# A pinned instruction order carried on into batch 2 and arranged anew, with tile addresses from a list: slot attention and a GELU feed-forward layer on one core

## The chip, the core and the metric

The kernel runs on one NeuronCore of a Trainium2 chip. The core has a matrix engine (TensorE, PE in the rows, PEld for its weight loads), a vector engine (VectorE, DVE), a scalar engine (ScalarE, ACT), GpSimd (POOL) and SyncE (SP). Here SP issues nearly all DMA transfers. The metric is the device time of one execution in microseconds (us); less is better. The time of a kernel is the median of its runs.

## The reference

```python
# batch 8, heads 8, seq 576, head_dim 64, n_mem 32; float32, the weights float64
a = phi - np.max(phi, axis=2, keepdims=True)          # over seq
a = np.exp(a)
a = a / (np.sum(a, axis=2, keepdims=True) + 1e-09)
k_m = np.einsum('bhsm,bhsd->bhmd', a, k)
v_m = np.einsum('bhsm,bhsd->bhmd', a, v)
scores = (1.0 / np.sqrt(64)) * np.matmul(q, k_m.transpose(0, 1, 3, 2))
scores = scores - np.max(scores, axis=-1, keepdims=True)
attn = np.exp(scores)
attn = attn / (np.sum(attn, axis=-1, keepdims=True) + 1e-09)
x = np.matmul(attn, v_m)           # -> (4608, 512), heads side by side
h = x @ w_in                       # w_in (512, 2048)
g = 0.5 * h * (1.0 + erf(h / np.sqrt(2.0)))
out = g @ w_out                    # w_out (2048, 512)
```

The weights reach the core as 64-bit numbers, in two 32-bit halves, and are turned into float32 there.

## The kernel before

Each batch is 576 tokens. The attention part makes, per batch, a softmax over the sequence, 32 slots for each head (k_m and v_m) and the attention weights of the tokens over the slots. The feed-forward part never builds x: the slots v_m are first multiplied with w_in (tile U), and the hidden layer is attention weights times U. Every large product is made of three passes with operands split into a high and a low part (hi, lo).

The program is written as a list of small pieces. A piece is a name with numbers; `a`, `d` or `p` behind a colon puts it on ACT, DVE or POOL. The order of the pieces in the list is the order of the instructions on every engine, since a dependency is added from each instruction to the one before it on its engine. The pieces that the text speaks of:

- Loads, all on SP: `Lphi` (phi), `Lkv0`, `Lkv` (k and v), `Lq` (q), `Lwi.f` and `Lwo.f` (128 columns of w_in, 128 rows of w_out; f from 0 to 15). `os` stores a result.
- Softmax over the sequence, batch b, half of the heads g: `amax.b.g` (DVE), `aexp.b.g` (ACT), `anorm` (DVE), `at.b.g.c` (transposes on PE), `atc.b.g.c` (their copy out of PSUM).
- Slots: `slots.b.g` (PE), `km.b.g` (scaled copy), `slotsT` (PE), `kT` (copy). In batch 0 a third number says k (0) or v (1).
- Attention weights of batch 0, in three parts x: `n_score` (PE), `n_max`, `n_sub` (DVE), `n_exp` (ACT), `n_sum`, `n_inv`, `n_mul` (DVE), `n_T` (PE), `n_hi` (ACT), `n_lo` (DVE). In later batches `score`, `sT`, `max`, `sub`, `exp`, `sum`, `inv`, `mul`, `pT`, `ph`, `pl`.
- U: `Up.b.f.n` (PE), `Uh` (copy of the high part), `Ul` (DVE, the rest).
- Weights: `dB.f.k` (ACT, two instructions; k is 0 for w_in, 1 for w_out), `dC`, `dG`, `dS` (DVE), `dDi`, `dDo` (POOL), `dE` and `dF` (high and low part of w_out).
- Hidden layer: `h.b.f.hf` (PE, 6 matmuls, half the tokens), `gelu` (ACT), `gh` (high part, ACT or DVE), `gl` (low part, DVE), `p.b.f` (PE, 12 matmuls into acc), `o` (evict). From batch 2 on `P` and `O` with half batches. `tg`, `tp`, `to` do the same for the 64 tokens of a batch that are left over. `W` is a matmul whose result nobody reads.

`START` is the part of the list that is written out by hand; before, it ends with `p.1.15`, the last product of batch 1. What follows is put in order by a small planner (`put` with a due time, `run` after each `h`), which leaves out what `START` has done (`done`). `HOME` says which buffer (U0 to U4, kv0 to kv7, wy0, wy1) each big tile uses; a tile waits until the last reader of the tile that had the buffer before is through. Eight semaphores serve SP's transfers in turn, so that the ninth after a transfer isn't issued before that one has landed.

PE's names in the rows: pt = `at`, pk = `slots`, tn = `slotsT`, psc = `n_score` and `score`, pu = `Up`, pT = `n_T`, acc = `p`.

Of the kernel before, what the change touches and what calls it, by code (L numbers as in the profile page):

```python
# [50 lines left out]
n_max.1 n_sub.1 n_exp.1 n_mul.0 Lkv0.1.1 slots.0.1.1 Lphi.1.0 amax.1.0 n_sum.1 Lwi.2
km.0.1.1 Lphi.1.1 n_inv.1 n_mul.1 dDi.0 Lwo.2 slotsT.0.1 kT.0.1 aexp.1.0 Up.0.0.1
Lkv.1.0.0 dDi.1 dB.2.0 Uh.0.0:d Ul.0.0 dC.2.0 amax.1.1 aexp.1.1 dG.2.0 dS.2.0 Lkv.1.0.1
n_score.2 Up.0.1.1 Uh.0.1:d Lkv.1.0.2 Lwo.3 n_T.0 n_T.1 Ul.0.1 dDi.2 Lkv.1.0.3 n_max.2
n_sub.2 dB.2.1 dG.2.1 dC.2.1 at.1.1.0 dS.2.1 n_hi.0 at.1.0.0 Lkv.1.0.4 n_lo.0 h.0.0.0
atc.1.1.0 Lkv.1.1.0 atc.1.0.0:d at.1.0.4 n_exp.2 n_sum.2 n_inv.2 n_mul.2 atc.1.0.4:d
dB.3.1 n_hi.1 dC.3.1 dDo.2 dG.3.1 dS.3.1 dDo.3 anorm.1 at.1.1.4 n_T.2 atc.1.1.4
gelu.0.0.0 n_hi.2 Lwi.3 slots.1.0 km.1.0 Lkv.1.1.1 n_lo.2 n_lo.1 h.0.0.1 dB.3.0 dC.3.0
dS.3.0 dE.2 Up.0.2.1 Lkv.1.1.2 gelu.0.0.1 Lwo.4 Uh.0.2 Lkv.1.1.3 h.0.1.0 gelu.0.1.0
h.0.1.1 dG.3.0 dF.2 Ul.0.2 gh.0.0:a gl.0.0 dB.4.1 dC.4.1 dG.4.1 Lkv.1.1.4 slots.1.1  # L60
h.0.2.0 dS.4.1 km.1.1 slotsT.1 kT.1:d Lwi.4 dDi.3 Lwi.5 Lq.1.0 gelu.0.1.1 gh.0.1:a
dB.4.0 h.0.2.1 Up.0.3.1 p.0.0 gl.0.1 dE.3 dG.4.0 dDo.4 dE.4 dF.4 gelu.0.2.1 Uh.0.3
# [6 lines left out]
dG.6.1 dDi.6 Up.0.6.1 Uh.0.6 ph.1.0:d dC.7.1 h.0.5.0 h.0.5.1 dB.7.0 Ul.0.6 dC.6.1
max.1.1 dG.7.0 gelu.0.5.1 gelu.0.5.0 Up.1.0.4 Uh.1.0 dC.7.0 dS.7.0 sub.1.1 h.0.6.0  # L70
gelu.0.6.0 Lphi.2.1 dDi.7 amax.2.1 gh.0.5:a Ul.1.0 gl.0.5 pl.1.0 exp.1.1 dS.6.1 dDo.6
dE.6 h.0.6.1 gelu.0.6.1 p.0.4 Up.0.7.1 Uh.0.7:d sum.1.1 dS.7.1 inv.1.1 p.0.5 gh.0.6:a
Ul.0.7 Up.1.4.4 h.0.7.0 gelu.0.7.0 h.0.7.1 gelu.0.7.1 dG.7.1 Uh.1.4 mul.1.1 pT.1.1
ph.1.1:d dDo.7 dF.6 dB.8.1 h.1.0.0 gl.0.6 dE.7:d dF.7 p.0.6 dB.8.0 Lwo.9 dB.9.1 pl.1.1
# [1150 lines left out]
```

## Time and profile before

| | |
|---|---|
| median of 3 runs | 703.3 us (702.92 to 704.18) |
| the profiled execution | 704.61 us |
| its span, first to last instruction | 702.8 us |
| mean granted TensorE clock in it | 0.981 of full speed |
| busy in the span | PE 98%, PEld 82%, DVE 55%, ACT 42%, POOL 7% |

The span lies 1.81 us below the time of the same execution. A busy share is an average over the whole span; the first 40 us are quite different from the rest. Matmuls are pipelined and their ends are modelled, so how fast PE works is read from the distance of their starts.

### The profile page before, as it was taken

The numbers are of one execution on the slowest core, as the hardware profiler recorded it, in microseconds if no ns is written. First come the engines' busy times: TensorE is split into PE (matmuls) and PEld (weight loads), VectorE is DVE, ScalarE is ACT, GpSimd is POOL, SyncE is SP. The second block draws the span as 40 slices with busy tenths as digits, with TensorE's granted clock in tenths as the row PEclk, the third lists the DMA queues.
The fourth block names the chain that finished last, engine by engine and source line by source line (L and its number), as shares of the span: only waits on it lengthen the run. The fifth ranks groups of instructions, "written<-read, shape, count | busy, mean of one in ns | idle before, by whom it ended". The sixth has DMA issues, their size and how long they took to land.

```text
span 702.8 us, 12357 instructions
## 1 busy us (share of the span) xinstructions
PE 691.1 (98%) x4940; PEld 576.6 (82%) x4940; DVE 388.6 (55%) x705; ACT 298.4 (42%) x768; POOL 46.6 (7%) x39
## 2 busy tenths in 40 slices
PE   7999999999999999999999999999999999999997
PEld 5767787887878888888887888888877888888886
DVE  4989998954755366534943346433834346432222
ACT  4588766862615264524553224222531225322220
POOL 1232243310000000000000000000000000000000
PEclk7599999999999999999999999999999999999999
DMA  8954451416253571145600200020000200000001
GB/s 318 329 211 172 154 197 62 133 29 212 86 142 117 177 217 23 65 137 159 190 1 32 82 2 31 1 98 1 30 1 31 83 1 31 1 31 0 31 1 45
DMA packets 30716, 64.37 MB, mean 92 GB/s; under 512 B 3780, under 2 KB 8644, under 8 KB 30660
## 3 DMA queue, kind: packets, MB, share of 16 engines
q1 hardware_dynamic: 30564, 63.46, 27.6%
...
q10 hardware_dynamic: 96, 0.13, 0.1%
...
## 4 chain that ended last, share of the span: by engine, by line
PE 94%; DMA 1%; DVE 1%; SPq 0%; ACT 0%; issue 0%
PE acc L895 50%; PE h L855 29%; PE tacc L895 6%; PE pu L598 4%; PE psc L598 1%; PE psc L506 1%; DMA raw<-w_in 1%; PE pk L531 1%; PE x L506 1%; SPq L345 0%; PE pk L506 0%; PE psc L519 0%; PE psc L560 0%; DVE aT L210 0%; PE x L519 0%
## 5 line engine op out<-in xcount | busy, mean ns | idle before, releaser
L855 PE MATMUL h<-p_hi,U 128*128 128x288 f32 x1024 | 203.8, 298 | 0.0
L895 PE MATMUL acc<-wo_hi,gh 128*128 128x512 f32 x512 | 200.6, 392 | 0.0
L895 PE MATMUL acc<-wo_hi,gl 128*128 128x512 f32 x512 | 199.7, 390 | 0.0
L895 PE MATMUL acc<-wo_lo,gh 128*128 128x512 f32 x512 | 199.6, 390 | 0.0
L867 ACT ACTIVATE gf<-h 128x256 f32<-128x256 f32 x192 | 74.0, 387 | 265.0 <-issue 206.4
L855 PEld LDWEIGHTS h<-p_hi,U 128*128 128x128 f32 x1024 | 164.0, 188 | 23.0 <-issue 8.3
L210 DVE CAST gh<-gf 128x512 fp32r<-128x512 f32 x109 | 46.9, 430 | 167.4 <-ACT gf L867 165.3
L895 PEld LDWEIGHTS acc<-wo_hi,gh 128*128 128x128 f32 x512 | 96.5, 188 | 21.1 <-DVE gl L882 3.4
L895 PEld LDWEIGHTS acc<-wo_hi,gl 128*128 128x128 f32 x512 | 96.1, 188 | 21.5 <-DVE gl L882 0.9
L895 PEld LDWEIGHTS acc<-wo_lo,gh 128*128 128x128 f32 x512 | 96.1, 188 | 15.8
L855 PE MATMUL h<-p_lo,U 128*128 128x288 f32 x512 | 108.8, 294 | 0.1
L882 DVE TENSOR_TENSOR gl<-gf,gh 128x512 fp32r<-128x512 f32 x128 | 94.3, 736 | 15.2 <-ACT gh L210 5.7
L855 PEld LDWEIGHTS h<-p_lo,U 128*128 128x128 f32 x512 | 81.4, 188 | 0.6 <-DVE p_lo L693 0.6
L814 DVE TENSOR_TENSOR U<-pu,U 128x512 fp32r<-128x512 f32 (+2 forms) x50 | 40.8, 834 | 42.0 <-ACT U L210 41.8
L869 ACT ACTIVATE tails<-h 128x32 f32<-128x32 f32 x192 | 37.4, 195 | 0.0
L598 PE MATMUL pu<-w_in_sb,kT 64*32 64x512 f32 (+2 forms) x624 | 34.4, 528 | 0.4 <-ACT kT L210 0.4
L210 ACT CAST U<-pu 128x512 fp32r<-128x512 f32 (+2 forms) x42 | 30.4, 759 | 7.4 <-PE pu L598 7.3
L305 POOL TENSOR_TENSOR w_in_sb<-y,raw 128x512 int32<-128x512 int32 x16 | 23.8, 1493 | 43.8 <-DVE y L285 11.8
L305 POOL TENSOR_TENSOR y<-y,raw 128x512 int32<-128x512 int32 x16 | 21.9, 1374 | 56.5 <-DVE y L285 23.9
L272 ACT ACTIVATE y<-raw 128x512 f32<-128x512 f32 x32 | 21.6, 675 | 8.9 <-issue 4.3
L895 PE MATMUL tacc<-wo_hi,gh_t 128*128 128x512 f32 x64 | 25.0, 391 | 0.0
L895 PE MATMUL tacc<-wo_hi,gl_t 128*128 128x512 f32 x64 | 24.9, 389 | 0.0
...
## 6 DMA issues: line engine op xcount, KB each, us to landing
...
```

The source lines that it names most:

```text
L210: return e.copy(dst, src) if e is nc.scalar else e.tensor_copy(dst, src)
L272: nc.scalar.activation(y, high.bitcast(F32), AF.Abs, scale=2.0**16)
L305: nc.gpsimd.tensor_tensor(w, y, low, op=ALU.add)
L506: nc.tensor.matmul(pk[32 * j : 32 * j + 32, : 2 * D], st["aT", b][:, c, g, 32 * j : 32 * j + 32], st["kv", b, g, c][:, :, j, :], start=(c ...
L531: nc.tensor.matmul(pk[32 * j : 32 * j + 32, w0 * D : (w0 + n) * D], st["aT", b][:rows, c, g, 32 * j : 32 * j + 32], t[:rows, w0 : w0 + n, ...
L598: nc.tensor.matmul(ps[g][M * j : M * j + M], st["kT", b][rows, t, M * j : M * j + M], moving[j][rows], start=True, stop=True,)
L814: nc.vector.tensor_sub(u[:, ..., 1, :], pu, u[:, ..., 0, :].bitcast(F32))
L855: i = nc.tensor.matmul(h[:, :HS], u[g][w], x[:, g, :], start=(n == 0), stop=(n == 3 * G - 1))
L867: nc.scalar.activation(gf[:, f % 2 * n : f % 2 * n + n], h[:, :n], AF.Gelu)
L869: nc.scalar.activation(t, h[:, n:HS], AF.Gelu)
L882: nc.vector.tensor_tensor(g_of("gl", *k), g_of("gf", *k), g_of("gh", *k).bitcast(F32), op=ALU.subtract)
L895: nc.tensor.matmul(acc, x, w[:, f, :], start=(first and n == 0), stop=(last and n == 2))
```

## The change

`START` gets a new order from its first piece to `p.1.15` and goes on through the first half of batch 2 (850 pieces against 694). `PLACES` is new: a list of all tile tags with size and number of buffers, allocated in this order at the start, so that every tile has an address that doesn't depend on which piece comes first. `HOME` is the same. The pair `a_add`, `a_x` is now named apart, and the store `os` is a piece of its own and no longer the end of `o`. The entries of `st` that send some products to the accumulators' PSUM banks stand ahead of `START`, since it now reaches the pieces that use them. Over the whole program DVE has 675 rows for 685 and ACT 755 for 745: ten rows more move from DVE to ACT than back; PE's are the same ones in another order.

```diff
+PLACES = """
+kT:1024*3 phi:4608*1 nm:8*2 sm:8*2 aT:5120*1 rz:8*2 mx:72*2 smx:72*2 U0:8192*1 U4:8192*1
...
 START = """
-W.4.3 Lphi.0.0 amax.0.0 aexp.0.0 at.0.0.0 Lphi.0.1 amax.0.1 aexp.0.1 anorm.0 atc.0.0.0:d
...
+Lphi.0.1 Lphi.0.0 Lwo.0 Lkv0.0.0 Lkv0.1.0 Lq.0.0 Lwi.0 amax.0.0 Lwo.1 amax.0.1 aexp.0.1 Lq.0.1
...
+gl.0.0 km.1.1 dC.4.0 p.0.0 dB.4.1 dS.4.0 dC.4.1 gelu.0.1.0 dS.4.1 dG.3.0 amax.2.0 dDi.3
...
-    def first_tiles():
-
-        for tag in ("mx", "smx"):
-            sb.tile([P, G * SB], F32, tag=tag, name=f"{tag}_first")
+    for x in PLACES.split():
+        tag, size, n = x.replace("*", ":").split(":")
+        sb.tile([P, int(size) // 4], F32, tag=tag, name=f"place_{tag}", bufs=int(n))
...
-        if f == NF - 1 and j % 2:
-            r = b * S + (j - 1) * P
-            nc.sync.dma_start(
-                out[r : r + 2 * P, :].rearrange("(c p) n -> p c n", p=P), st["o", b, j // 2]
-            )
+
+    def store(b, j):
+        r = b * S + (j - 1) * P
+        nc.sync.dma_start(
+            out[r : r + 2 * P, :].rearrange("(c p) n -> p c n", p=P), st["o", b, j // 2]
+        )
```

First place: ACT at the start, behind its first table load and the load's exponential. phi is the softmax's input (`aexp`), aT the copy of a transpose (`atc`), y and raw the weights (`dB`), km the slots' copy. Before:

```order
L398 ACTIVATE phi_101,sm_105<-phi_101,nm_103 128x576 x2
L210 COPY aT_107<-pt_1_0_120 128x4x128
L272 ACTIVATE y_171<-raw_130 128x512
L273 ACTIVATE raw_130<-raw_130 128x512
L549 ACTIVATE km_201<-pk_0_144,rz_117 128x64
L549 ACTIVATE km_201<-pk_1_180,rz_117 128x64
```

and now:

```order
L414 ACTIVATE phi_136,sm_157<-phi_136,nm_152 128x576 x2
L288 ACTIVATE y_168<-raw_139 128x512
L289 ACTIVATE raw_139<-raw_139 128x512
L228 COPY aT_162<-pt_1_4_181 64x128
L228 COPY aT_162<-pt_1_0_163 128x4x128
L228 COPY aT_162<-pt_0_0_171 128x4x128
L561 ACTIVATE km_241<-pk_0_193,rz_217 128x64
L561 ACTIVATE km_241<-pk_1_219,rz_217 128x64
```

Two of the copies were DVE's, and all three now stand behind `dB.0.1`. The `x2` of the first row are `aexp.0.0`, `aexp.0.1` before and `aexp.0.1`, `aexp.0.0` now, while DVE has `amax.0.0`, `amax.0.1` in both and SP now loads group 1 first.

Second place: PE between the scores of batch 0 and the first products of U (`slots.0.g.1`, `slotsT.0.1`, `n_score.2`, `Up`). Before:

```order
L295 MATMUL warm_251<-one 128x128
L531 MATMUL pk_0_144<-kv_0_135,aT_107 32x64 x16
L531 MATMUL pk_0_144<-kvt_0_136,aT_107 32x64 x4
L531 MATMUL pk_1_180<-kv_1_139,aT_107 32x64 x16
L531 MATMUL pk_1_180<-kvt_1_140,aT_107 32x64 x4
L560 MATMUL tn_215<-ident,km_201 128x128
L598 MATMUL pu_0_330<-w_in_sb,kT_217 32x128 x8
L615 MATMUL psc_2_355<-k_blocks,q_1_169 128x2x32 x4
L598 MATMUL pu_1_360<-w_in_sb,kT_217 32x128 x8
```

and now:

```order
L543 MATMUL pk_1_219<-kv_1_145,aT_162 32x64 x16
L543 MATMUL pk_1_219<-kvt_1_146,aT_162 32x64 x4
L543 MATMUL pk_0_193<-kv_0_141,aT_162 32x64 x16
L543 MATMUL pk_0_193<-kvt_0_142,aT_162 32x64 x4
L627 MATMUL psc_2_357<-k_blocks,q_1_159 128x2x32 x4
L572 MATMUL tn_246<-ident,km_241 128x128
L610 MATMUL pu_0_386<-w_in_sb,kT_250 32x128 x8
```

`n_score.2` (psc_2) has moved ahead of `slotsT.0.1` (tn), and the unread matmul (warm) has moved to an earlier place. Behind this PE now has `n_T.0`, `Up.0.1.1`, all of `at.1`, `n_T.1`, the two short transposes, `h.0.0.0`, `slots.1.0`, `n_T.2`, `Up.0.2.1`, `h.0.0.1`, `slots.1.1`, `h.0.1.0` and then `p.0.0`; before, `h.0.1.1`, `h.0.2.0`, `slotsT.1`, `h.0.2.1` and `Up.0.3.1` still stood ahead of `p.0.0`, and `n_T.2` and the short transposes ahead of `slots.1.0`.

Third place: ACT and DVE up to the first low part, gl_0 (`gl.0.0`); gf and tails are `gelu`, gh is `gh`, p_hi_1 from pT_2 is `n_hi.2`, p_lo_1 from pT_2 is `n_lo.2`. ACT before:

```order
L873 ACT_TABLE_LOAD
L873 ACTIVATE gf_0_455<-h_0_0_415 128x288
L689 CAST p_hi_1_438<-pT_2_451 128x64 x2
L549 ACTIVATE km_481<-pk_0_460,rz_448 128x2x64
L272 ACTIVATE y_435<-raw_372 128x512
L273 ACTIVATE raw_372<-raw_372 128x512
L210 CAST wo_hi<-y_343 128x512
L875 ACTIVATE gf_0_455<-h_1_0_489 128x224
```

and now:

```order
L561 ACTIVATE km_526<-pk_0_495,rz_461 128x2x64
L701 CAST p_hi_1_486<-pT_2_528 128x64 x2
L885 ACT_TABLE_LOAD
L885 ACTIVATE gf_0_559<-h_0_0_473 128x288
L887 ACTIVATE gf_0_559<-h_1_0_548 128x224
L888 ACTIVATE tails<-h_1_0_548 128x64
L228 CAST gh_0_589<-gf_0_559 128x512
```

DVE now, from `n_lo.2` to `gl.0.0`:

```order
L705 TENSOR_TENSOR p_lo_1_487<-pT_2_528,p_hi_1_486 128x64 x2
L228 CAST U_0_395<-pu_2_535 128x2x128
L826 TENSOR_TENSOR U_0_395<-pu_2_535,U_0_395 128x2x128
L408 TENSOR_REDUCE nm_557<-phi_480 128x1
L228 CAST wo_hi<-y_364 128x512
L327 TENSOR_TENSOR wo_lo<-y_364,wo_hi 128x512
L293 TENSOR_SCALAR y_381<-y_381 128x512
L301 TENSOR_SCALAR y_381<-y_381 128x512
L894 TENSOR_TENSOR gl_0_606<-gf_0_559,gh_0_589 128x512
```

The table load and the first `gelu` stand behind `km.1.0` and `n_hi.2`, where they stood ahead of both. On DVE `Uh.0.2`, `amax.2.1` and `dE.2` are new between `n_lo.2` and `gl.0.0`.

## Rows read from the trace of the kernel before

**Rows 1.** The page: busy times, and the granted clock in 40 slices (tenths).

```profile
PE 691.1 (98%) x4940; PEld 576.6 (82%) x4940; DVE 388.6 (55%) x705; ACT 298.4 (42%) x768; POOL 46.6 (7%) x39
PEclk7599999999999999999999999999999999999999
```

**Rows 2.** Windows: stretch, length, busy time (instructions) by engine, granted clock, DMA share, GB/s.

```profile
0.00:10.20 10.20, 6.59 (x54) 5.86 (x57) 4.33 (x12) 5.04 (x9) 0.95 (x7) 1.00 0.80 255
10.20:34.10 23.90, 21.36 (x246) 17.65 (x234) 18.67 (x41) 11.14 (x26) 6.85 (x5) 0.50 0.96 350
34.10:37.50 3.40, 2.02 (x10) 1.01 (x8) 3.30 (x10) 2.70 (x8) 1.31 (x1) 1.00 0.35 142
37.50:41.00 3.50, 3.49 (x44) 2.63 (x45) 1.73 (x8) 2.74 (x7) 1.29 (x1) 0.51 0.34 118
41.00:60.00 19.00, 19.00 (x206) 14.82 (x205) 18.32 (x35) 16.95 (x37) 6.38 (x5) 1.00 0.81 297
60.00:80.00 20.00, 20.00 (x167) 14.34 (x166) 19.62 (x40) 14.98 (x30) 6.73 (x5) 1.00 0.13 41
```

**Rows 3.** The chain that ended last: start, length, what (two of its `p` groups).

```profile
47.40 2.99 PE acc L895 x12
...
244.77 2.72 PE acc L895 x12
```

**Rows 4.** Timeline, the start: start, length, instruction, idle time before and its releaser.

```profile
4.37 0.78 ACT L398 ACTIVATE phi<-phi,nm 128x576 f32<-128x576 f32 x1 [2.14 <-DVE nm L392]
4.59 0.75 DVE L392 TENSOR_REDUCE nm<-phi 128x1 f32<-128x576 f32 x1 [0.25 <-DMA phi<-phiT]
...
7.22 0.58 ACT L210 COPY aT<-pt 128x512 f32<-128x512 f32 x1 [0.97 <-PE pt L423]
...
9.83 0.78 PE L531 MATMUL pk<-kv,aT 128*32 128x64 f32 x32 [2.43 <-DMA kv<-kv]
...
15.07 7.06 PE L615 MATMUL psc<-k_blocks,q 128*128 128x64 f32 x32 [0.72 <-ACT k_blocks L210]
```

**Rows 5.** Timeline from the scores of batch 0 to the first hidden product.

```profile
22.59 1.08 PE L531 MATMUL pk<-kv,aT 128*32 128x64 f32 x32
...
26.57 0.27 ACT L210 COPY kT<-tn 128x128 f32<-128x128 f32 x1 [0.57 <-PE tn L560]
...
27.59 1.97 PE L615 MATMUL psc<-k_blocks,q 128*128 128x64 f32 x8
...
30.95 0.66 ACT L272 ACTIVATE y<-raw 128x512 f32<-128x512 f32 x1
...
32.08 0.68 ACT L689 CAST p_hi<-pT 128x288 fp32r<-128x288 f32 x2
...
33.57 0.76 PE L855 MATMUL h<-p_hi,U 128*128 128x288 f32 x2
...
34.50 0.42 ACT L646 ACTIVATE s<-s 128x256 f32<-128x256 f32 x1
```

**Rows 6.** Timeline from the slots of batch 1 on.

```profile
37.48 1.28 ACT L873 ACT_TABLE_LOAD   x1
37.51 2.52 PE L531 MATMUL pk<-kv,aT 128*32 128x128 f32 x40
38.77 0.41 ACT L873 ACTIVATE gf<-h 128x288 f32<-128x288 f32 x1
39.08 0.32 ACT L689 CAST p_hi<-pT 128x64 fp32r<-128x64 f32 x2
39.96 0.85 PE L855 MATMUL h<-p_hi,U 128*128 128x288 f32 x2
...
41.38 0.45 PE L598 MATMUL pu<-w_in_sb,kT 64*32 64x128 f32 x16
41.76 0.53 PE L855 MATMUL h<-p_hi,U 128*128 128x288 f32 x2
...
43.59 1.43 PE L531 MATMUL pk<-kv,aT 128*32 128x128 f32 x40
44.95 0.53 PE L855 MATMUL h<-p_hi,U 128*128 128x288 f32 x2
```

More of the change, by code (lines that the diff above doesn't have):

```diff
@@ L51 @@
[L51 to L62, printed above, removed]
@@ L69 @@
[L69 to L74, printed above, removed]
@@ new lines @@
+aexp.0.0 at.0.1.0 dB.0.1 at.0.0.0 dC.0.1 W.4.3 at.0.0.4 at.0.1.4 dS.0.1 Lwi.1 atc.0.1.4:a
+dG.0.1 atc.0.1.0 atc.0.0.0:a Lkv0.1.1 atc.0.0.4:d dDo.0 slots.0.0.0 dE.0:d W.4.13 anorm.0
+slots.0.1.0 dF.0 km.0.0.0 Lkv0.0.1 km.0.1.0 slotsT.0.0 W.3.29 kT.0.0 n_score.0 dB.0.0 Lwi.2
+dC.0.0 dG.0.0 dB.1.1 Lphi.1.0 dC.1.1 dS.1.1 dG.1.1 n_score.1 dS.0.0 dDo.1 n_max.0 n_sub.0
+dDi.0 n_exp.0 dE.1:a n_sum.0 dB.1.0 Lwo.3 dF.1 slots.0.1.1 Lwi.3 dC.1.0 Lphi.1.1 n_max.1 Lwo.2
+slots.0.0.1 dS.1.0 km.0.1.1 Lkv.1.1.2 dG.1.0 Lkv.1.0.0 n_inv.0 dDi.1 n_score.2 Lkv.1.0.3
@@ new lines @@
+dB.2.0 n_sub.1 amax.1.0 Lkv.1.0.4 km.0.0.1 dC.2.0 n_exp.1 slotsT.0.1 n_mul.0 Lkv.1.1.0 kT.0.1
+dB.3.1 n_sum.1 Up.0.0.1 n_T.0 dC.3.1 Lkv.1.0.2 n_inv.1 Uh.0.0:a aexp.1.0 Ul.0.0 Lwi.4 n_max.2
+Up.0.1.1 amax.1.1 n_sub.2 Uh.0.1:a Lkv.1.0.1 dS.3.1 aexp.1.1 Ul.0.1 Lkv.1.1.1 n_exp.2 n_mul.1
+at.1.0.0 dB.2.1 Lwo.4 dS.2.0 dC.2.1 at.1.1.0 dG.3.1 atc.1.0.0:a n_T.1 dG.2.0 atc.1.1.0 anorm.1
+n_hi.0 dDi.2 at.1.1.4 at.1.0.4 n_lo.0 h.0.0.0 Lphi.2.1 atc.1.0.4:a atc.1.1.4 n_sum.2 n_hi.1
+dDo.3 n_lo.1 dB.3.0 slots.1.0 n_inv.2 dS.2.1 Lkv.1.1.3 dE.3 n_mul.2 Lkv.1.1.4 dG.2.1 km.1.0
@@ new lines @@
+n_T.2 Lwo.5 n_hi.2 Up.0.2.1 Lphi.2.0 n_lo.2 dDo.2 h.0.0.1 Uh.0.2:d Ul.0.2 amax.2.1 gelu.0.0.0
+slots.1.1 Lwo.6 gelu.0.0.1 dE.2:d Lwi.5 gh.0.0:a dF.2 Lq.1.0 h.0.1.0 dC.3.0 dB.4.0 dS.3.0
+gl.0.0 km.1.1 dC.4.0 p.0.0 dB.4.1 dS.4.0 dC.4.1 gelu.0.1.0 dS.4.1 dG.3.0 amax.2.0 dDi.3
+slotsT.1 kT.1:d h.0.1.1 dF.3 Lwo.7 Up.0.3.1 dG.4.0 gelu.0.1.1 gh.0.1:a h.0.2.0 dG.4.1 dDi.4
+Uh.0.3 h.0.2.1 Ul.0.3 gelu.0.2.0 gl.0.1 dB.5.1 score.1.0 dDo.4 dB.5.0 p.0.1 sT.1.0.1 sT.1.0.0
+max.1.0 gelu.0.2.1 Lwo.8 dE.4 dC.5.0 Lwi.6 dC.5.1 gh.0.2:a Lq.1.1 sub.1.0 Lwi.8 Up.0.4.1
@@ L1000, in slot_attention_gelu_ffn @@
     }
+    st.update({("far", "pu", b, f): 1 for b in range(3, B) for f in (4, 12)})
+    st.update({("far", "psc", b, 1): 1 for b in range(3, B)})
+    st.update({k: 1 for k in (("far", "xt", 3), ("far", "pu", 2, 12))})
     done = set()
@@ L1167, in slot_attention_gelu_ffn @@
             if end:
-                behind += [f"o.{b}.{j}.{f}" for j in range(NT)]
+                for j in range(NT):
+                    behind += [f"o.{b}.{j}.{f}"]
+                    if f == NF - 1 and j % 2:
+                        behind += [f"os.{b}.{j}"]
         else:
```

124 lines of the change are left out of this document (66 added, 58 removed).

## The prediction

> **What bounds the kernel now.** I read the page first: PE is busy for 98% of the span, and its clock is below full speed in the first slices only [rows 1]. Since ends of matmuls are modelled, a busy PE need not be a fast one, so I looked next at the windows and at the distance of starts. From 41 us on PE has no idle time in any window and the granted clock is full [rows 2]. One `p` group of 12 matmuls takes 2.99 us at 47 us and 2.72 us at 245 us [rows 3]: there is some friction while the weights are decoded, and none later. So behind 41 us there is nothing to wait for that a better order could take away. It can only add waits there.
>
> The gain has to come from the first 41 us, and the windows show what they look like. From 10.2 to 34.1 us the clock is granted at half (1.2 GHz), 3.4 us are at full speed, and from 37.5 to 41 us it is half again [rows 2]; PE had paused for `h.0.0.0` and the transposes ahead of the second fall. In this part DVE is the engine with the least air: busy 18.67 of 23.9 us from 10.2 on, 3.30 of 3.40 us from 34.1 on, and 19.62 of 20 us between 60 and 80 us [rows 2]. So PE and DVE are close to each other for the first 90 us, and the time is set by when PE's steady stream begins and whether DVE then keeps ahead of it. The pieces behind p.1.15 and all of batch 2 lie in the part without waits: that `START` reaches further, that stores are pieces of their own and that addresses come from a list I cost at nothing, hidden behind a PE that is never idle; if that cover were gone, a store or a load costs its place on SP only.
>
> **The start, up to the scores.** Before, the first `aexp` begins at 4.37 us and the second `amax` at 4.59 us, when the second load has landed [rows 4]. Now group 1 is loaded first, but DVE still takes `amax.0.0` first, which has to wait for the second load; ACT takes `aexp.0.1` first. So ACT starts at 4.59 + 2 x 0.75 = 6.1 us, and two exponentials of 0.78 us end at 7.7 us, where before the second ended at about 4.59 + 0.75 + 0.78 = 6.1 us: 1.6 us later. Before, the last long copy ended at 7.22 + 0.58 = 7.8 us, and `slots.0.0.0` still waited until 9.83 us for its load [rows 4]. Now there are 1.6 us more, and two copies that DVE did beside ACT stand in ACT's row (0.58 us and a short one of about 0.3), all behind `dB.0.1`: 7.8 + 1.6 + 0.9 = 10.3 us at least. I take 11.1, because the copy that is needed is the last of the three and the first of them waits for the last short transpose. The cover by the load is used up, and PE is 1.3 us late. I give back 0.2 us, an estimate, for the unread matmul that no longer stands ahead of `slotsT.0.0`. So the scores start at 16.2 us for 15.07 us [rows 4].
>
> **From the scores to the first hidden product.** The two scores take 7.06 us [rows 4], to 23.2 us. Before, it took 3.98 us from the first of the two `slots` to `kT.0.1` (22.59 to 26.57 us); now `n_score.2` stands between (1.97 us) and covers the pause for `km` (I take 0.8 us of it): `kT.0.1` comes at 28.3 us for 26.57 us [rows 5]. Behind it ACT has `dB.3.1`, whose first half (0.66 us) releases DVE's `dC.3.1`, `n_inv.1`, `Ul.0.0`, `n_max.2` and `amax.1.1`: six instructions at DVE's mean in this stretch, 18.67 / 41 = 0.46 us [rows 2], together 2.7 us. Then ACT has `aexp.1.1` (0.78 [rows 4]), `n_exp.2` (0.42), `dB.2.1` (two halves, 1.2), two copies (1.1) and `n_hi.0` (0.68) [rows 4, 5]: 4.2 us. With kT's own 0.27 us that is 7.8 us, so `h.0.0.0` starts at 36.1 us, 2.5 us later than the 33.57 us of before [rows 5].
>
> Most of this comes back at once. Before, the short transposes and `n_T.2` stood between `h.0.0.0` and `slots.1.0`, which began at 37.51 us [rows 6]. Now only the low part stands there: two DVE instructions (0.9 us) and the last two matmuls, so `slots.1.0` begins at about 37.3 us. At half clock it takes 39.96 - 37.51 = 2.45 us [rows 6], and `n_T.2` behind it about 0.5 us, an estimate: at 40.2 us PE has done what it had done at 39.96 us before. **First term: +0.2 us.** Its bounds are -1.3 us (no lag at the start: the exponentials aren't on the path) and +1.2 us (the copies and `n_score.2` counted whole).
>
> **The first product.** `p.0.0` now comes four small pieces behind `n_T.2`: `Up.0.2.1` (0.38 us), `h.0.0.1` (two `h` took 43.59 - 41.76 us, 0.91 each), `slots.1.1` (44.95 - 43.59 = 1.36) and `h.0.1.0` (0.91) [rows 6]: 3.6 us at full clock, 4.0 us with the first of it at half. It needs `gl.0.0`, and that needs two branches from `n_T.2` on. On ACT: `n_hi.2` 0.32, the table load 1.28, `gelu.0.0.0` 0.41 [rows 6], then `gelu.0.0.1` and `gh.0.0` at about 0.5 each: 3.0 us. On DVE, after `n_hi.2` (0.4 us with its wait): ten instructions, of which the two of `n_lo.2` are short; I take nine at 19.62 / 40 = 0.49 us [rows 2], 4.4 us. DVE's branch ends last, at 4.8 us, and PE stands for 0.8 us. Behind `gl.0.0` on DVE are all later low parts, so the stall isn't won back. **Second term: +0.8 us**; its bounds are 0 (DVE does most of it ahead of time) and +1.5 us.
>
> For the table load a page differs from the row. Here it takes 1.28 us, and the first `gelu` starts right at its end, at 38.77 us [rows 6]. The Trainium skill (ScalarE: Activation LUTs, section What ACT_TABLE_LOAD costs) adds a drain of about 1.38 us to a load of 1283 ns. By that, ACT's branch would be the later one, 4.4 us and `gl`'s half microsecond, and the stall 0.1 to 0.3 us longer. The row decides.
>
> **Behind it.** From `gl.0.0` to `gl.0.7` DVE has 66 instructions, by 0.49 us 32.3 us. PE has meanwhile seven `p` at 2.85 us (between the two of [rows 3]), 13 `h`, five short and one long `Up`, two scores: 20.0 + 11.8 + 1.9 + 1.0 + 1.3 = 36 us. DVE is ahead at each product, by 0.8 us at `p.0.1` and 1.1 us at `p.0.3`, where it is tightest. **Third term: 0**, with up to +2.5 us if DVE has to wait itself.
>
> **The sum.** 0.2 + 0.8 = +1.0 us. The profiled execution's 704.61 us becomes 705.6 us; it lies 1.3 us above the median of the runs, so the median goes from 703.3 to 704.3 us. A measurement of this kernel tells about 0.2% (1.4 us) from no change, so my forecast is: no difference that can be measured, on the slow side.
>
> **Rivals.**
>
> *DVE doesn't keep ahead (slower).* The margins at `p.0.1`, `p.0.3` and `p.0.6` are about 1 us each, out of 3.7 us in all. They hold if DVE never waits. Before, with hidden products ahead of the first `p`, it worked without pause; but from 37.5 to 41 us it was idle for half the time [rows 2], waiting for ACT, and now the first `p` begins right there. If DVE waits for ACT for 5.5 us of the 36, PE loses 5.5 - 3.7 = 1.8 us more: 706.1 us. It decides from 3.7 us of idle time on. For it speaks that ACT gets the moved copies and was busy for 16.95 of 19 us [rows 2]; against it that these are taken from DVE.
>
> *Fewer instructions on DVE pay (faster).* Up to the first hidden product DVE has six instructions less (four copies, two casts), 6 x 0.46 = 2.8 us. If the start is DVE's alone, as 3.30 of 3.40 us busy suggest [rows 2], my chain through ACT has slack that I don't see, and 1.8 of the 2.8 us reach PE: 703.3 - 1.8 = 701.5 us. Against it speaks that DVE was busy for only 78% from 10.2 to 34.1 us [rows 2]. The Trainium skill (Perfetto Trace Analysis, section Optimizing Scalar/DVE Operations) says that with a saturated DVE moving work to Scalar may make sense, which would be this case; behind 41 us the trace shows no PE wait that it could shorten.
>
> *The clock stays full (no change).* With PE in a denser row from `h.0.0.0` on, the second stretch at half speed might not come. That saves 2.45 - 1.36 on `slots.1.0` and 0.5 us on one `h`, 1.6 us, but the cover of `p.0.0` shrinks by 0.5 us: 704.3 - 1.1 = 703.2 us. What PE did ahead of the first rise, at 34.1 us, was a row of transposes without pause; now there is a pause between them.
>
> *The order is the same for PE's purposes (no change).* The pieces ahead of the first `h` hardly differ, and all lags are covered: 703.3 us.
>
> **How the numbers follow.** Within 0.2%: my sum 0.22, the clock 0.09, nothing 0.11, together 0.42. DVE behind: 0.33. DVE's relief: 0.25. The range goes to the two other cases and half a microsecond past the slow one, since the bounds of the terms add up on that side: 701.2 to 706.6 us; 1 in 10 is left out at each end.
>
> **What would show it.** In the changed profile I expect ACT's first `aexp` at 6.1 us, the first psc at 16.2 us, `kT.0.1` at 28.3 us, the first `h` at 36.1 us, `slots.1.0` at 37.3 us, and PE idle for some 0.8 us ahead of the first acc, which begins at about 45 us, released by DVE's gl. I am wrong if the first acc begins before 44 us, if the clock is granted at full speed before 30 us, or if PE is idle for over 1 us in sum between 50 and 250 us: then a step behind the start, which I cost at nothing, matters.

## The result and the profile after

The changed kernel takes 708.27 us (median of 6 runs, 707.33 to 710.70), beside 703.93 us for the kernel before. The ratio is 1.0067, 95% interval 1.0046 to 1.0087. A second series of the same kernel (e18 below) gave 707.15 us and 1.0054, 1.0037 to 1.0070. So the change makes the kernel 0.5 to 0.7% slower. I had forecast 704.3 us and no measurable difference; both series lie above my range. The profiled execution took 708.27 us with a span of 706.5 us, 3.7 us more than before.

The page of the changed kernel, for [rows 1]:

```profile
PE 689.3 (98%) x4940; PEld 573.6 (81%) x4940; DVE 379.8 (54%) x694; ACT 301.7 (43%) x779; POOL 45.1 (6%) x39
PEclk8599999999999999999999999999999999999999
```

PE has the same 4940 instructions, the span is longer, and PE's busy time is 1.8 us less: it stands still for longer. By the two pages eleven rows have moved from DVE to ACT. The windows, with the columns of [rows 2], say where:

```profile
10.20:34.10 23.90, 19.95 (x257) 16.02 (x257) 17.27 (x42) 15.03 (x34) 5.28 (x5) 0.57 0.95 348
37.50:41.00 3.50, 3.10 (x65) 2.08 (x63) 2.77 (x7) 3.20 (x8) 1.29 (x1) 1.00 0.91 291
41.00:60.00 19.00, 18.36 (x167) 13.96 (x166) 18.75 (x36) 16.30 (x34) 7.14 (x5) 1.00 0.75 277
60.00:80.00 20.00, 19.57 (x150) 14.65 (x135) 18.78 (x36) 15.62 (x33) 5.37 (x4) 1.00 0.23 74
220.00:240.00 20.00, 17.47 (x217) 14.34 (x220) 11.85 (x25) 7.91 (x21) 0.00 (x0) 1.00 0.61 176
```

From 37.5 to 41 us the clock is now full. From 41 to 80 us PE, which had no idle time there, has 1.1 us of it, and from 220 to 240 us, deep in batch 2, 2.5 us. The waits of PE from 41 to 300 us (in all, times, longest) name what it waited for; before, this answer was empty:

```profile
PE psc L518 <- DMA kv<-kv: 1.8, 1, 1.8
PE h L867 <- ACT gf L885: 0.8, 1, 0.8
PE pu L610 <- DVE U L826: 0.8, 2, 0.4
PE psc L610 <- ACT kT L228: 0.8, 1, 0.8
PE pu L610 <- POOL w_in_sb L321: 0.2, 1, 0.2
```

These are 4.4 us, more than the loss in span. So the start must have won something. The timeline of the start, for [rows 4 to 6]:

```profile
5.75 0.77 ACT L414 ACTIVATE phi<-phi,nm 128x576 f32<-128x576 f32 x1 [3.51 <-DVE nm L408]
10.71 1.08 PE L543 MATMUL pk<-kv,aT 128*32 128x64 f32 x32 [1.31 <-ACT aT L228]
15.75 5.37 PE L627 MATMUL psc<-k_blocks,q 128*128 128x64 f32 x32 [0.50 <-issue]
26.03 0.27 ACT L228 COPY kT<-tn 128x128 f32<-128x128 f32 x1
34.04 0.85 PE L867 MATMUL h<-p_hi,U 128*128 128x288 f32 x2
38.12 1.28 ACT L885 ACT_TABLE_LOAD   x1
39.42 0.41 ACT L885 ACTIVATE gf<-h 128x288 f32<-128x288 f32 x1
41.83 0.69 DVE L894 TENSOR_TENSOR gl<-gf,gh 128x512 fp32r<-128x512 f32 x1
41.87 0.40 PE L907 MATMUL acc<-wo_hi,gh 128*128 128x512 f32 x1
42.58 0.50 PE L907 MATMUL acc<-wo_hi,gl 128*128 128x512 f32 x1
```

The scores take 5.37 us where they took 7.06, and `h.0.0.0` comes at 34.04 us, where I had it at 36.1.

The two orders do different pieces at a given time, so I compare them **at equal work**: every matmul of a trace counts with the mean distance to the next start that its kind has behind 130 us in the kernel before; this is added up along PE's row; and I read off when each kernel has done what the kernel before had done at 45, 90, 105, 200 and 260 us. Minus is ahead of it. Behind 260 us nothing changes any more in any kernel.

```
order run                            45     90    105    200    260
e1  old order, changed code       -0.40  -0.36  -0.33  -0.33  -0.33
changed kernel                    -1.80  -0.21  +0.70  +0.05  +3.67
e18 changed kernel again          -3.05  -1.43  -1.51  -2.15  +1.25
e2  new to p.1.15, planner        -1.86  -0.31  -0.41      (a wait of its own)
e3  slots.4 later                 -0.12  +1.44  +1.80  +1.28  +4.59
e5  and ax.4 later                -0.06  +1.49  +1.44  +0.88  +3.54
e6  planner from slots.3          -1.95  -0.35  +0.46  -0.06  +4.64
e10 batch 2 mended                -1.94  -0.13  +1.34  +0.70  +2.18
e16 and Lwi.11 earlier            -0.57  +1.01  +0.90  +0.38  +1.87
e4  new start, old rest           -0.22  +0.85  +0.87  +0.89  +0.89
e9  the same, joined earlier      -0.52  +0.98  +1.03  +1.02  +1.02
e13 changed, light dG             -3.02  -2.21  -2.18  -2.82  -0.02
e17 e16, light dG                 -0.56  +0.21  +0.12  +0.24  +1.73
e14 old order, light dG           -1.60  -1.69  -1.77  -1.74  -1.74
e15 changed, light dB             -2.00  -0.65  -0.75  -1.27  +1.76
```

Lines 2 to 9 have the same order up to 75 us and more. Their start is 0.1 to 3.1 us ahead (mean 1.4), the middle from 45 to 90 us costs 1.55 to 1.81 us in every one, the stretch around 100 us -0.1 to +1.5 us, the rest up to 200 us gives back 0.6 us, and batch 2 costs 3.4 and 3.6 us in the two executions of the unaltered kernel. Their mean around 100 us is +0.4. -1.4 + 1.6 + 0.4 - 0.6 + 3.5 = +3.5 us; between the medians there are 4.3 and 3.5 us.

The start is the uncertain part of this sum, since it goes with the clock. In e3, e5 and e16 PE works at half speed up to 36.5 us and more, and they are 0.1 to 0.6 us ahead; the other five have a stretch at full clock in the first 21 us and are 1.8 to 3.1 us ahead. The old order's executions differ too (e1 -0.40; e14, with a lighter piece on DVE, -1.60), and the one that all are compared with here took 0.7 us more than the median of its series.

**Batch 2.** The timeline of the changed kernel around the wait (SPq rows are issues on SP), and below it links of the chain of waits (start, length):

```profile
221.19 1.96 PE L518 MATMUL x<-kv,aT 128*32 128x128 f32 x64
222.77 0.33 SPq L361 DMA_DIRECT2D kv<-kv  x1
223.67 1.27 SPq L450 DMA_DIRECT2D aT<-phiN  x1
231.42 1.28 ACT L491 ACT_TABLE_LOAD   x1 [2.85 <-DMA aT<-phiN]
232.72 1.17 ACT L491 ACTIVATE aT<-aT 128x1152 f32<-128x1152 f32 x1
233.91 1.28 ACT L879 ACT_TABLE_LOAD   x1
235.56 0.44 ACT L228 COPY kT<-xt 128x128 f32<-128x128 f32 x2
236.05 1.21 PE L610 MATMUL psc<-q,kT 64*32 64x288 f32 x32 [0.76 <-ACT kT L228]
```

```profile
226.74 6.69 DMA kv<-kv
...
233.45 5.44 DMA kv<-kv
238.89 0.14 issue
239.03 1.95 PE psc L518 x64
```

The row at 221.19 us is `slots.3`. k and v of batch 4 go into the buffers that it reads, and so does phi of batch 4 (`Lphin.4`); their first issue is at 222.77 us, right when `slots.3.1` lets go, and the last lands at 233.45 + 5.44 = 238.9 us, 17.7 us after `slots.3` began. From the start of `slots.3` to that of `slots.4` the new list has 239.03 - 221.19 = 17.8 us, of which 2.5 us are the two waits: 15.3 us of work, 2.4 too few. ACT meets `ax.4` first and stands for 2.85 us for `Lphin.4`; its exponential takes a table load on either side, `kT.3` is queued behind it, and `score.3` waits for that. In the kernel before the planner put 21.0 us between the two, as its timeline shows (`slots.3`, then `slots.4`):

```profile
228.33 1.96 PE L506 MATMUL x<-kv,aT 128*32 128x128 f32 x64
...
249.33 1.96 PE L506 MATMUL psc<-kv,aT 128*32 128x128 f32 x64
```

The order of the loads may have a part in the lateness as well. On SP three loads of batch 5 (issued at 223.15, 228.32 and 231.35 us) stand between those of batch 4, and the last one of batch 4 is issued at 233.45 us, when the eighth transfer before it, issued at 226.74 us, has landed. In the kernel before, with no load of batch 5 between, the DMA engines were through at 244.8 us, 16.5 us after `slots.3` began. By these figures 15.3 us of work would still be 1.2 us too few, an estimate from one execution; a list with the loads in that order was not run.

**Around 100 us** the same happens with a weight: issues of q and of w_in (`Lwi.11`), then ACT at `dB.11.0`, with the `gelu` that h needs queued behind:

```profile
90.05 0.43 SPq L395 DMA_DIRECT2D q<-qT  x1
90.53 0.42 SPq L267 DMA_DIRECT2D raw<-w_in  x1
99.10 0.68 ACT L288 ACTIVATE y<-raw 128x512 f32<-128x512 f32 x1 [3.18 <-DMA raw<-w_in]
100.69 0.53 PE L867 MATMUL h<-p_hi,U 128*128 128x288 f32 x2 [0.81 <-ACT gf L885]
```

### The profile page after: what moved, and what is told of

Its sections match the earlier page's. It is cut to its first block, busy times and chain, and to the rows that moved or that the text cites. A ratio compares the mean times of both kernels' runs of the same rounds, so it can differ in the third digit from the quotient of the medians.

```text
span 706.5 us, 12335 instructions
## 1 busy us (share of the span) xinstructions
PE 689.3 (98%) x4940; PEld 573.6 (81%) x4940; DVE 379.8 (54%) x694; ACT 301.7 (43%) x779; POOL 45.1 (6%) x39
## 4 chain that ended last, share of the span: by engine, by line
PE 85%; DMA 7%; DVE 4%; SPq 2%; issue 1%; ACT 1%; POOL 0%; ACTq 0%; POOLq 0%; DVEq 0%
PE acc L907 45%; PE h L867 27%; PE tacc L907 6%; PE pu L610 4%; DMA kv<-kv 3%; DMA raw<-w_out 2%; DMA raw<-w_in 1%; DMA q<-qT 1%; PE psc L610 1%; PE psc L518 1%; DVE raw L297 1%; DVE gl L894 1%; PE x L518 0%; DVE y L293 0%; SPq L267 0%
## 5 line engine op out<-in xcount | busy, mean ns | idle before, releaser
L228 DVE CAST gh<-gf 128x512 fp32r<-128x512 f32 x101 | 43.1, 426 | 161.2 <-ACT gf L879 156.1
L894 DVE TENSOR_TENSOR gl<-gf,gh 128x512 fp32r<-128x512 f32 x128 | 89.4, 699 | 34.4 <-ACT gh L228 24.9
L881 ACT ACTIVATE tails<-h 128x32 f32<-128x32 f32 x192 | 37.5, 195 | 0.0
L228 ACT CAST U<-pu 128x512 fp32r<-128x512 f32 (+2 forms) x42 | 28.5, 709 | 7.0 <-PE pu L610 7.0
L321 POOL TENSOR_TENSOR w_in_sb<-y,raw 128x512 int32<-128x512 int32 x16 | 21.9, 1370 | 49.3 <-DVE raw L297 30.2
```

Source lines behind the costliest of these rows:

```text
L228: return e.copy(dst, src) if e is nc.scalar else e.tensor_copy(dst, src)
L321: nc.gpsimd.tensor_tensor(w, y, low, op=ALU.add)
L881: nc.scalar.activation(t, h[:, n:HS], AF.Gelu)
L894: nc.vector.tensor_tensor(g_of("gl", *k), g_of("gf", *k), g_of("gh", *k).bitcast(F32), op=ALU.subtract)
```

## Experiments

Where not said otherwise a kernel is the changed one with some pieces of `START` in other places. Expectations that speak of 708.3 us speak of the changed kernel. The kernel before was timed beside each group, with medians from 703.5 to 704.4 us.

**e1: is it the order?**

```diff
 START = """
-Lphi.0.1 Lphi.0.0 Lwo.0 Lkv0.0.0 Lkv0.1.0 Lq.0.0 Lwi.0 amax.0.0 Lwo.1 amax.0.1 aexp.0.1 Lq.0.1
+W.4.3 Lphi.0.0 amax.0.0 aexp.0.0 at.0.0.0 Lphi.0.1 amax.0.1 aexp.0.1 anorm.0 atc.0.0.0:d
...
```

> The old order of START in the changed kernel: the list of addresses, the separate store pieces and the early far entries stay, the order of the pieces is that of before. If the time lies in the order alone: 703.9 us, ratio to before 1.000 within 0.002. If the addresses or the stores cost something: up to 707 us, with the same rows of work ahead of the first acc as in before.

703.88 us, ratio 1.0003 (0.9992 to 1.0014). Addresses, store pieces and the early `far` entries cost nothing. All that follows is the order.

**e2, e6: batch 2 back to the planner.** e2 keeps of the new order the pieces that the old `START` had; e6 ends it ahead of `slots.3`; the diff is that of e6.

```diff
 sub.2.1 Lq.3.0 h.2.2.0 mr.4 Uh.2.8:d h.2.3.0 gelu.2.2.0 Ul.2.8 h.2.4.0 P.2.0.0 exp.2.1
-gelu.2.3.0 h.2.5.0 slots.3.0 gelu.2.5.0 gelu.2.4.0
...
+gelu.2.3.0
```

> The new order only for the 697 pieces that the old START had too; the rest (most of batch 2) goes back to the planner. If the pinned part of batch 2 costs its own stalls (0.8 us ahead of score.3 and 1.8 us ahead of slots.4 in the profile, 3.0 us by the curve at equal work): 708.3 - 3.0 = 705.3 us, with no PE wait between 200 and 260 us. If the late loads come from what is done ahead of batch 2 instead, the planner meets the same late loads and it stays at about 708 us.

> The changed START up to gelu.2.3.0, just ahead of slots.3; from there the planner, which puts slots.3 and slots.4 some 18 us of PE work apart (13.9 us in the changed kernel). If the pinned distance is what costs: no PE wait behind 205 us, 708.3 - 3.3 = 705.0 us. If the loads are late whatever the distance: still 707 us or more.

(The 13.9 and 18 us are rough counts of the PE work between the two; the rows above give 15.3 and 21.0 us from start to start.)

e2: 716.34 us, 1.0184 (1.0168 to 1.0200). e6: 709.10 us, 1.0069 (1.0052 to 1.0086). Both cuts made a wait of their own, which I hadn't seen: in e2 the softmax of `score.2.1` stood on DVE ahead of batch 1's evictions, in e6 ahead of `gh.2.0.1`. PE's waits, of e2 and then of e6:

```profile
PE tacc L890 <- DVE o L954: 8.1, 1, 8.1
```

```profile
PE acc L894 <- DVE gh L215: 1.9, 1, 1.9
```

As times they decide nothing. But behind their wait (from 210 and from 225 us) neither curve rises any more, e6 stands at +4.60 at 225 and at +4.64 from 230 us on: with the planner's distance (`slots.3` at 232.97 us, `slots.4` at 253.97 us) `slots.4` doesn't wait.

**e3, e5, e10: the waits of batch 2 one after the other.**

The diff is that of e10; e3 moves `slots.4.0`, `slots.4.1`, `km.4.0` and the loads behind them alone, e5 these and `ax.4`.

```diff
-Lkv.4.0.1 mul.2.1 aadd.4 P.2.0.3 Lkv.4.0.4 Lkv.4.0.0 Ul.2.12 ax.4 pT.2.1 h.2.8.0 slotsT.3
-gelu.2.8.0 h.2.9.0 kT.3 score.3.1 gelu.2.9.0 score.3.0 gh.2.0.4:a sT.3.1.1 slots.4.0 sT.3.1.0
-Lkv.5.0.0 ph.2.1:d slots.4.1 gl.2.0.4 Lkv.5.1.1 Lkv.5.0.2 P.2.0.4 km.4.0 Lphin.5 Lkv.5.0.3
...
+Lkv.4.0.1 mul.2.1 aadd.4 P.2.0.3 Lkv.4.0.4 Lkv.4.0.0 Ul.2.12 pT.2.1 h.2.8.0 slotsT.3
+gelu.2.8.0 h.2.9.0 kT.3 score.3.1 gelu.2.9.0 score.3.0 gh.2.0.4:a ax.4 sT.3.1.1 sT.3.1.0
+ph.2.1:d h.2.10.0 gelu.2.10.0 h.2.11.0 gl.2.0.4 P.2.0.4 Lphin.5
...
+P.2.0.5 slots.4.0 slots.4.1 km.4.0 Lkv.5.0.0
```

> The changed kernel with slots.4.0, slots.4.1, km.4.0 and the loads of batch 5 that follow them moved behind P.2.0.5, two products further on (some 10 us). If PE waits there for the loads of batch 4 only because it comes too early: the 1.8 us wait is gone, the 0.8 us ahead of score.3 stays, 708.3 - 1.8 to 2.2 = 706.3 us. If the loads' lateness moves on (the transfers of batch 5 are then later too and something else waits): 708 us or more, with a new DMA wait behind 250 us.

> As e3, and ax.4 (an exponential on ACT that waits for the load Lphin.4, with a table load ahead of it and one behind it) moved behind gh.2.0.4. In the changed kernel and in e3 ACT stands for 2.8 us ahead of ax.4 and is then taken by it until 235 us, with kT.3 and two gelu queued behind. If the loss between 225 and 240 us is ACT waiting for that load, and slots.4 for the loads of batch 4, both issued only when slots.3 has let go of its buffers: both waits are gone, 708.3 - 3.0 = 705.3 us. If the loss only moves on again, as in e3: 707.5 us or more.

> As e5, and h.2.10.0 and h.2.11.0 moved ahead of P.2.0.4, so that gl.2.0.4 has cover where e5 let PE wait 0.9 us for it. If the loss of batch 2 is made of these waits (loads of batch 4 for slots.4, ACT waiting for Lphin.4, gl.2.0.4) and of nothing else: 708.3 - 2.7 = 705.6 us and no PE wait behind 205 us. If it is borne by the placing of the other pieces too: 707 us.

e3: 708.36 us, 1.0073 (1.0060 to 1.0085): no gain. The load wait is gone, but `slots.4` had been the cover for `gl.2.0.4`, late behind `ax.4` on ACT, and PE now waits there. e5: 707.96 us, 1.0054 (1.0039 to 1.0069): ACT no longer stands, but PE still waits 0.7 us for `gl.2.0.4`. e10, with two h as cover: 706.10 us, 1.0038 (1.0026 to 1.0050), 2.2 us less than the changed kernel's first series and 1.1 less than its second. From 200 to 260 us it loses 1.5 us for 3.4 to 3.6. So two of the 3.5 us are these waits, and a mend counts only when the cover that it takes away is given back. The other 1.5 us are no waits of PE that the trace names; 0.9 of them lie between 200 and 225 us, ahead of the moved pieces, and the changed kernel loses the same 0.9 us there in both executions.

**e4, e7, e9: is the early start real?** e4 and e9 take the new order up to `p.0.0`, with and without it, and the old order behind; e7 the old order up to `p.0.0` and the new one behind. The diff is that of e9, against e4, at the join.

```diff
 dF.2 Lq.1.0 h.0.1.0 dC.3.0 dB.4.0 dS.3.0 gl.0.0 km.1.1 dC.4.0
-p.0.0
 gelu.0.1.0 h.0.1.1 dG.3.0 dB.4.1 dC.4.1 dG.4.1 h.0.2.0 dS.4.1 slotsT.1
...
 h.0.2.1 Up.0.3.1
+p.0.0
 gl.0.1 dG.4.0 dDo.4 dE.4 dF.4 gelu.0.2.1 Uh.0.3 Ul.0.3 score.1.0
```

> The new order up to and with p.0.0, then the old order for all that is left, then the planner as before. At p.0.0 the changed kernel is 1.8 to 2.0 us ahead of the one before at equal PE work. If that lead is real: 703.9 - 1.9 = 702.0 us. If it is borrowed (vector and scalar work for the next products left undone), the lead is gone by 75 us here as in the changed kernel, and the time is 703.5 to 705 us.

> As e4, but the join stands ahead of p.0.0: the new order up to h.0.1.0, then the old one, in which p.0.0 stands between Up.0.3.1 and score.1.0 and covers the U piece on ACT and DVE. In e4 PE waited 1.4 us there for Ul.0.3 and 1.0 us for a load of k and v. If the lead of the new start is real and e4 lost it in the join: 703.6 - 1.0 = 702.7 us. If any old rest behind the new start pays it back (DVE and ACT are not ahead, only PE is): 703.6 to 705 us.

> The other half of e4: the old order up to and with p.0.0, then the new order for all that is left. If the 1.6 us that the changed kernel loses between 45 and 90 us at equal work are the repayment of its early start: they don't occur here, and only the part at 225 to 240 us does: 703.7 + 3.3 = 707.0 us. If they belong to the new order of the middle itself: 703.7 + 1.6 + 3.3 = 708.6 us.

e4: 704.81 us, 1.0018 (1.0009 to 1.0028); e9: 704.93 us, 1.0019 (1.0008 to 1.0030). Their starts were 0.2 and 0.5 us ahead in the profiles; by 60 us 1.0 and 1.5 us were lost, at other places each time (e4: 1.4 us for U on DVE and 1.0 us for a load; e9: 0.9 us for `kT` on DVE). So PE's lead at `p.0.0` wasn't a lead of DVE, ACT and the loads in these two lists. How much of the loss is a join's own, as in e7 below, and how much the repayment of a borrowed lead, they don't tell apart. e7: 712.69 us, 1.0120 (1.0101 to 1.0139); PE waits 2.6 us for U at 50 us, right at the join. It fits neither expectation, and since the join alone costs over 5 us it says nothing about the middle.

**e8, e11, e12: the waits of the middle.** Up.0.5.1 waits at 57 us; ACT has been through two exponentials with a table load at 52.04 and another at 54.80 us, and reaches the high part of the U piece ahead of it at 56.4 us. The timeline:

```profile
54.80 1.28 ACT L885 ACT_TABLE_LOAD   x1
56.40 0.37 ACT L228 CAST U<-pu 128x256 fp32r<-128x256 f32 x1
57.02 0.36 DVE L826 TENSOR_TENSOR U<-pu,U 128x256 fp32r<-128x256 f32 x1
57.53 0.45 PE L610 MATMUL pu<-w_in_sb,kT 64*32 64x128 f32 x16 [0.36 <-DVE U L826]
```

The diff is that of e11. e8 instead takes `amax.2.1` and `amax.2.0` from their places ahead of `gelu.0.0.0` and `slotsT.1` to one behind `sub.1.1`, and `aexp.2.1` from ahead of `p.0.2` to behind `exp.1.1`.

```diff
-gl.0.2 Lwi.7 h.0.3.0 Lphin.2 dG.5.1 exp.1.0 h.0.3.1 dF.4 aexp.2.1 dS.5.0 p.0.2 dG.5.0 sum.1.0
-dDi.5 gelu.0.3.0 Uh.0.4:a inv.1.0 gelu.0.3.1 Ul.0.4 dB.6.0 mul.1.0 Up.0.5.1
+gl.0.2 Lwi.7 h.0.3.0 Lphin.2 dG.5.1 exp.1.0 h.0.3.1 dF.4 aexp.2.1 Uh.0.4:d Ul.0.4 dS.5.0 p.0.2
+dG.5.0 sum.1.0 dDi.5 gelu.0.3.0 inv.1.0 gelu.0.3.1 dB.6.0 mul.1.0 Up.0.5.1
...
-Up.1.0.4 dG.7.0 dDo.6 sum.1.1 gelu.0.6.0 p.0.5 Uh.1.0 inv.1.1 dC.7.1 dDi.7 Ul.1.0 dS.7.1
+Up.1.0.4 Uh.1.0 dG.7.0 dDo.6 sum.1.1 gelu.0.6.0 p.0.5 inv.1.1 Ul.1.0 dC.7.1 dDi.7 dS.7.1
...
-dC.10.0 dB.11.0 dS.10.0 h.1.4.0 dG.10.1 dDi.10 h.1.4.1 dC.11.0 gelu.1.4.0 gh.1.3:a h.1.5.0
-gelu.1.4.1 gh.1.4:a gl.1.3
+dC.10.0 dS.10.0 h.1.4.0 dG.10.1 dDi.10 h.1.4.1 gelu.1.4.0 gh.1.3:a h.1.5.0
+gelu.1.4.1 gh.1.4:a dB.11.0 dC.11.0 gl.1.3
```

> The changed kernel with amax.2.1 and amax.2.0 (0.73 us each on DVE, between n_lo.2 and the second product) moved behind sub.1.1 at about 65 us, and aexp.2.1 to the place of aexp.2.0. If DVE's own work is what holds up gl and the U pieces between 42 and 60 us: PE gets about 1 us of the 1.6 us back, 707.3 us. If ACT or the loads set the pace there, or if DVE pays it back at 65 us: 708.3 us.

> The changed kernel with four pieces of the middle moved: Uh.0.4 to DVE and with Ul.0.4 ahead of dS.5.0, Uh.1.0 right behind Up.1.0.4 and Ul.1.0 ahead of dC.7.1, dB.11.0 and dC.11.0 behind gh.1.4. In the changed kernel Up.0.5.1 and Up.0.7.1 wait 0.4 and 0.5 us for U pieces that ACT reaches late, behind exponentials with a table load on either side, and h.1.5.0 up to 1.0 us because ACT stands at dB.11.0 for its load. If that is the loss of the middle: 708.3 - 1.4 = 706.9 us. If DVE's work sets the pace anyway: 708.3 us.

> The edits of e10 and e11 together. If the losses are separate waits, they add up: 708.3 - 2.7 - 1.4 = 704.2 us. If not, about 706 us.

e8: 711.41 us, 1.0106 (1.0088 to 1.0124), 3 us above the changed kernel: nothing won before 60 us, and with the exponential moved into the second block on ACT the wait at 74 us grew from 0.4 to 1.2 us. e11: 709.17 us, 1.0080 (1.0058 to 1.0101): no gain. The two U waits went, and in their place PE waited for w_in on POOL and for gl:

```profile
PE acc L904 <- DVE gl L891: 1.0, 3, 0.6
PE pu L607 <- POOL w_in_sb L318: 0.8, 2, 0.7
```

One of these is my edit's: `dC.11.0`, which I moved along, let DVE stand ahead of `gl.1.3`. e12, with e10's edits: 706.74 us, 1.0045 (1.0031 to 1.0058), 0.6 us above e10. From 45 to 90 us e11 and e12 lose 2.0 us each, for 1.6. My list of single waits as the cause of the middle's loss fell here.

**e13, e14, e15, e17: whose work sets the pace of the middle?**

The diff is that of e13, e14 and e17; e15 has the like for the low words in `dB`.

```diff
     def dec_g(f, *k):
         low, high = raw_half(f, k)
+        low, high = low[..., :64], high[..., :64]
```

> The changed kernel with dG, the copy of the sign bits, on 64 of 512 columns only: the signs of the other weights are left out, DVE has some 0.6 us less for each of 32 pieces, the order is the same. If DVE's decode work sets the pace of the new order from 45 to 105 us: the 1.5 us of the middle and part of the start come back, 708.3 - 2 = 706.3 us or less. If single waits for ACT and the loads do: 708 us.

> The control for e13: the old order with the same light dG. Behind 41 us the old order has no PE wait, so that only the start can gain: 703.0 to 703.6 us. If it gains as much as the new order does, DVE's work isn't what tells the two orders apart.

> The changed kernel with the second instruction of dB (ACT, the low words) on 64 of 512 columns: the low words of the other weights stay unscaled, ACT has some 0.5 us less for each of 32 pieces. If ACT, which takes exponentials with table loads between the products in the new order, sets the pace from 45 to 75 us: 706.5 us. If DVE does: 708 us.

> e16 with the light dG of e13 (the signs of most weights are left out). Its control is e14, the old order with the same light dG (703.6 us). If DVE's work is what e16 still loses in the middle: 705.6 - 1.0 to 1.5 = 704.4 us, within 0.15% of e14. If something else is left: 705.6 us.

e13: 707.95 us, 1.0062 (1.0040 to 1.0083). e14: 703.56 us, 1.0000 (0.9989 to 1.0011). e15: 708.76 us, 1.0069 (1.0049 to 1.0089). e17: 705.17 us, 1.0021 (1.0012 to 1.0031), 0.4 us below e16. As times, these runs can't be told from those of the same order with the full pieces: the intervals overlap. The curve is clearer, with one execution each: from 45 to 90 us the light dG loses 0.81 us (e13) and 0.77 us (e17) where the eight of lines 2 to 9 lose 1.55 to 1.81; the old order loses nothing in either form; light dB loses 1.35. The stretch from the start of `gl.0.0` to that of `gl.0.7`, with the columns of [rows 2], in the changed kernel and in e13:

```profile
41.83:79.05 37.22, 36.15 (x292) 27.01 (x291) 35.78 (x67) 30.41 (x64) 12.52 (x9) 1.00 0.46 168
```

```profile
40.61:77.02 36.41, 35.95 (x291) 26.99 (x290) 31.51 (x68) 30.23 (x64) 12.24 (x9) 1.00 0.47 173
```

In the changed kernel DVE stands still for 1.4 of 37.2 us, with the light dG for 4.9 of 36.4. So DVE's work is half of the middle's loss, by the two light forms. ACT's part would be about 0.2 us, which one execution does not show for sure. The other half stays open.

**e16: the load at 100 us.**

```diff
-Lwo.11 dS.9.1 h.1.2.0 mw.2 Ul.1.4 dDo.9 Lq.2.0 h.1.2.1 Lwi.11
+Lwo.11 dS.9.1 h.1.2.0 Lwi.11 mw.2 Ul.1.4 dDo.9 Lq.2.0 h.1.2.1
```

> e10 with the load Lwi.11 ahead of mw.2 and Lq.2.0 on SP. If the wait of up to 1.5 us at 100 us is this load's place behind the big load of q: 706.1 - 0.7 = 705.4 us. If the load is late for another reason (its buffer, the semaphore of the eighth load before it): 706.1 us.

705.61 us, 1.0028 (1.0017 to 1.0040), 0.5 us below e10, with intervals that overlap. This execution has no wait at 100 us; but e5 and e18 have none either, with the load in its old place, so the edit isn't shown to be the reason. PE's waits from 41 to 300 us are these:

```profile
PE pu L607 <- DVE U L823: 0.8, 2, 0.5
PE pu L607 <- POOL w_in_sb L318: 0.2, 1, 0.2
PE acc L904 <- DVE gl L891: 0.2, 1, 0.2
```

It is the fastest form of the new order that I have, and still 0.28% slower than the kernel before. I found no order that beats the kernel before.

**e18: the changed kernel again.**

> The changed kernel itself, unaltered, for a second profile and more runs. 708.3 us, with the wait at 235 to 239 us again; its size goes with the landing of the loads of batch 4, 1.2 to 2.2 us. At 45 us it is 2.0 us or 0.1 us ahead of the kernel before, as its clock falls late or early in the first 16 us; from 45 to 90 us it loses 1.55 to 1.60 us as in five executions of this order. If the wait takes the clock down in this execution, the products behind it run at 427 ns for 227 ns and it is 2 us longer.

707.15 us, 1.0054 (1.0037 to 1.0070). The wait is there, 1.9 us for the loads and 0.5 for `kT`, the middle loses 1.62 us, the load at 100 us came in time. The clock didn't fall behind the wait, so this run doesn't show that the spread of the times comes from there.

## Why the prediction was wrong, step by step

**The first term (+0.2 us) was mis-sized, since I took one clock for granted.** My chain for the start is that of an execution in which PE stays at half speed up to 36.5 us. In e3, where all scores of the start came at 213 ns, `aexp` starts at 6.25, psc at 16.56, `kT.0.1` at 28.52 and `h.0.0.0` at 36.12 us; I had said 6.1, 16.2, 28.3 and 36.1. Such executions are 0.1 to 0.6 us ahead at 45 us (e3, e5, e16). In the others PE goes through a part of the slots or scores at full speed, which [rows 4] didn't show: the scores take 5.37 us in the changed kernel, and the start is 1.8 to 3.1 us ahead. What decides between the two isn't shown. Of the rivals, the one in which the clock stays full held from 37.5 to 41 us.

**The second term (+0.8 us) was too large.** DVE's branch took what I had said: ten pieces from 38.14 to 42.52 us, 4.4 us, so that `gl.0.0` ended 4.8 us behind `n_T.2` (37.70 us). PE's branch was longer: it took 4.2 us to `p.0.0` at 41.87 us, where I had 3.6 to 4.0, and I had overlooked that the first two matmuls of `p.0.0` read `gh` and not `gl`. Only the third, which reads `gl`, came late, by 0.25 us.

**The third term (0) failed in its price for DVE.** I took the 66 pieces of DVE from `gl.0.0` to `gl.0.7` at 0.49 us, 32.3 us beside 36 us of PE, and so had DVE ahead by 3.7 us. They are 66, but they took 37.2 us (41.83 to 79.05 us), 0.56 each, and no margin was left. The term is +1.6 us from 45 to 90 us, inside its bound of 2.5; with lighter pieces on DVE half of it goes (e13, e17). The rival's 1.8 us is near it by luck: it needed 3.7 us in which DVE waits for ACT, and DVE was idle for 1.4 us. I hadn't counted ACT's two blocks of exponentials with table loads, which stand in front of the U pieces that PE waits for; but e11, which took these waits away, won nothing.

**The step that decided is the one at nothing.** "That `START` reaches further ... I cost at nothing, hidden behind a PE that is never idle." PE was never idle before, since a planner kept 21.0 us from `slots.3` to `slots.4`; the list keeps 15.3 us, and loads that may start only when `slots.3` lets its buffers go needed 17.7. Batch 2 so cost 3.4 and 3.6 us from 200 to 260 us, the largest part of the loss, and 2.0 of them went with these waits (e10). That "a store or a load costs its place on SP only" was wrong for loads into a buffer that is still read: these cost the time until they have landed. I worked out the new order around `p.0.0` and not the distances of the pieces that release and reuse a buffer. Addresses and stores did cost nothing (e1). My own sign for this step (over 1 us of PE idle between 50 and 250 us) is what the trace shows. The first acc ahead of 44 us came too (41.87 us). The third sign, a full clock before 30 us, told nothing: the kernel before has it as well, from 6.8 to 10.2 us.

Open are half of the middle's loss (0.8 us) and 1.5 us of batch 2 in which PE has no named wait.

For the table load the row stays against the Trainium skill (ScalarE: Activation LUTs, section What ACT_TABLE_LOAD costs): in the changed kernel too it takes 1.28 us from 38.12 us, and the next `gelu` begins at 39.42 us, with no drain of 1.38 us.
